# Splitting the first chunk of a fused attention and mixture kernel in two, with the second chunk between the halves

## The chip, the cores and the metric

The kernel runs on one core of a Trainium2 chip. The metric is the device time of one execution in microseconds (us). The core's engines are TensorE (PE, with its weight loads shown as PEld), VectorE (DVE), ScalarE (ACT), GpSimd (POOL) and SyncE (SP, which issues most DMA transfers). Each works through its own queue in order.

## The reference

Three stages follow each other on 4 x 576 = 2304 tokens of width 512:

```python
scores = scale * np.matmul(q, k.transpose(0, 1, 3, 2))     # 4 batches, 8 heads, 576 x 576
scores = np.where(masks[None], scores, -1e9)               # heads 0-3: a band of 32; heads 4-7: every 32nd position
attn = exp(scores - max) / (sum + 1e-9);  x = attn @ v     # -> (2304, 512)
h = x @ w_in;  g = h * sigmoid(1.702 * h);  x = g @ w_out  # first mixture, d_ff 2048
# second mixture: 8 experts with d_ff 1024, each token goes to its top 2
noisy = x @ w_gate + log1p(exp(x @ w_noise)) * noise
out[mask] += top2_w * (relu(x[mask] @ w1[e]) @ w2[e])
```

Everything is float32. Products on TensorE are taken as three products of a rounded part ("hi") and a rest ("lo"): hi*hi, hi*lo, lo*hi.

## The kernel before

**Prologue.** Attention is cut into 64 groups, ordered in parts of 14, 14, 4, 14, 14 and 4; part c is what chunk c of the first mixture needs beyond the earlier parts. "Local" groups are of the banded heads (three masks of 128 x 96), "strided" groups of the others (two masks of 126 x 126 or 72 x 72). A group passes through `scores` (PE; then the mask with its row maximum on DVE, L169), `exps` (ACT, L174), `norms` (L178 and L180 on DVE, then the division: L182 on POOL for the first 28 groups, L186 on DVE for later ones), `transposes` (PE; then an ACT copy, L235 or L240) and `values` (PE, L252 or L262; then hi on ACT, L190, and lo on DVE, L193). The prologue works on groups one after another, a step apart, until all but one of part 0 have left `values`; by then 17 groups have been through `scores`, and six pieces of weights are converted.

**Chunks and slices.** The first mixture then runs in 6 chunks of 384 tokens, each in 16 slices of 128 of the 2048 hidden columns. A slice has 12 matmuls of its first layer (`m1_l1`), a tanh (ACT L416), the gate product (DVE L418), its split into hi (ACT L423) and lo (L425: POOL in chunk 0, DVE later), and 9 matmuls of the second layer of the slice before (`m1_l2`), which add up in the banks PB[2] to PB[4] over the 16 slices. Between the layers come the attention groups of the next part, one per slice: first half of a slice `values`, `transposes`, `scores`, `exps`, then `norms`; second half `values` and `transposes` again. After a chunk, `routing` scales the banks by 0.5 into rows, sends them to DRAM, transposes them, forms the logits and writes the expert lists; its steps are taken from a queue called `fill` at fixed places of the following slices.

**Weights.** Chunk 0 also converts the weights. They arrive as 64-bit words, two 32-bit words each. Of the 16 slices, 0 to 13 come in two wide pieces of 512 words each, 14 and 15 in four small pieces of 256 words each. `w_step` takes up to 512 words: three DVE instructions (`w_bits`, L387, L390, L393) build the float bits, and a step later `w_split` takes hi on ACT (L362) and lo on POOL (L363) and fetches the next raw piece. There are two such steps in each slice, so a slice converts both of its pieces. All four compute engines have their order written out by hand.

**Buffers.** The pool `wp` has 14 buffers. It holds the converted weights of slices 0 to 13, which stay until chunk 5, and the loads and scratch of "early" attention groups (groups 0 to 19 here), up to 8 groups ahead of `scores`. The instruction that first writes a new tile waits until the last reader of the tile that had the buffer is done. Later groups use the pools `ldp` and `tmp`, two ahead. Loads of early groups and of raw weights form one chain on SP, in order. Small pieces use three `stp` and two `tmp` buffers, at most five at a time, and are touched no sooner than LATE half slices after their fetch.

Of the kernel before, what the change touches and what calls it, by code (L numbers as in the profile page):

```python
# [9 lines left out]
F32 = mybir.dt.float32  # L10
F32R = mybir.dt.float32r
BF16 = mybir.dt.bfloat16
I32 = mybir.dt.int32
AF = mybir.ActivationFunctionType
OP = mybir.AluOpType
# [7 lines left out]
DM = H * D  # L23
FF = 2048
NFC = FF // 128
# [4 lines left out]
NCHUNK = N // CH  # L30
TPC = CH // 128
# [18 lines left out]

R_LG = 400
WAIT0 = 14
LATE = 3
REM = 1
CONVAT = (4, 6, 8, 10, 12, 14)
WAIT1 = 15
R_PP = R_LG + 16 * TPC
# [40 lines left out]
def tile_kernel(ctx, tc, qkL, qkS, vL, vS, wm1, wm2, wgn, noise, cst, lst0, out):  # L98
    nc = tc.nc
# [4 lines left out]
    PB = [psum.tile([128, 512], F32, tag=f"pb{i}", name=f"pb{i}") for i in range(8)]  # L104
# [13 lines left out]
    with ExitStack() as main, tc.manual_schedule(engines={mybir.EngineType.PE}):  # L118
# [205 lines left out]
        SPLIT = [[], []]  # L324
# [18 lines left out]
                SMALL.extend((fc, s, o, 256) for o in (0, 256))  # L343

        def w_small():
            while SMALL and len(held) < 5:
                fc, s, o, n = SMALL.pop(0)
                held.append(o)
                if (4 * fc + 2 * s + o // 256) % 5 < 3:
                    raw = stp.tile([128, n, 2], I32, tag="raw", name="raw")  # L350
                else:
                    raw = tmp.tile([128, n, 2], I32, tag="row", name="raw")
                a = 512 * s + o
                chained(raw.rearrange("p n t -> p (n t)"), wm1[fc, :, a:a + n].bitcast(I32))
                PIECES.append((fc, s, raw, o, n))
                born.append(len(done))

        def w_split():

            for fc, s, w32, o, n in SPLIT.pop(0):  # L360
                hi, lo = W1[fc, s]
                nc.scalar.copy(hi[:, o:o + n], w32)  # L362
                nc.gpsimd.tensor_sub(lo[:, o:o + n], w32, hi[:, o:o + n].bitcast(F32))  # L363
                if n < 512:
                    held.pop()
                else:
                    w_raw(fc + 2, s)
            w_small()
            SPLIT.append([])
            done.append(0)  # L370

        def w_step():
            left = 512
            while PIECES and left:
                fc, s, raw, o, n = PIECES[0]
                if n < 512:
                    if len(done) < born[0] + LATE:
                        return
                    born.pop(0)
                PIECES.pop(0)  # L380
                left -= n
                yield from w_bits(fc, s, raw, o, n)

        def w_bits(fc, s, raw, o, n):
            t = tmp.tile([128, n], I32, tag="cv", name="cv", bufs=1)
            low, high = raw[:, :, 0], raw[:, :, 1]
            nc.vector.tensor_scalar(t, high, 3, 0x3FFFFFFF,  # L387
                                    op0=OP.logical_shift_left, op1=OP.bitwise_and)
            yield
            nc.vector.scalar_tensor_tensor(low, low, 29, t,  # L390
                                           op0=OP.logical_shift_right, op1=OP.bitwise_or)
            yield
            nc.vector.scalar_tensor_tensor(low, high, -0x40000000, low,  # L393
                                           op0=OP.bitwise_and, op1=OP.bitwise_or)
            SPLIT[-1].append((fc, s, low.bitcast(F32), o, n))
            yield


        GT = {}
        LASTMM = [None]  # L400

        def m1_l1(c, fc, mid, conv):
            w = W1[fc, 0]
# [17 lines left out]

        def m1_split(c, t, g):
            nc.scalar.copy(g[:, 0], t)  # L423
            eng = nc.vector if c else nc.gpsimd
            eng.tensor_sub(g[:, 1], t, g[:, 0].bitcast(F32))  # L425

        def m1_l2(c, fc, mid):
            w = W1[fc, 1]
            g = GT.pop((c, fc))
            for t in range(TPC):  # L430
                if t == 1:
                    mid()
                o = PB[2 + t]
                a = slice(128 * t, 128 * t + 128)
                nc.tensor.matmul(o, g[:, 0, a], w[0], start=(fc == 0), stop=False)  # L435
                nc.tensor.matmul(o, g[:, 0, a], w[1], start=False, stop=False)  # L436
                m = nc.tensor.matmul(o, g[:, 1, a], w[0], start=False, stop=(fc == NFC - 1))  # L437
            LASTMM[0] = m.ins


# [1 line left out]

        def routing(c, tb, lb, wait=3):
            last = c == NCHUNK - 1
            if last:
                rows = wp.tile([128, TPC, DM], F32, tag="w", name="rows")
                xts = wp.tile([128, TPC, 4, 128], F32, tag="w", name="x2ts")
                row = [rows[:, j, :] for j in range(TPC)]
                xt = [xts[:, j] for j in range(TPC)]
            else:  # L450
                row = [tmp.tile([128, DM], F32, tag="row", name="row") for j in range(2)]
                row.append(stp.tile([128, DM], F32, tag="raw", name="row"))
                xt = [stp.tile([128, 4, 128], F32, tag="raw", name="x2t") for j in range(TPC)]
            for j in range(TPC):
                if j == 1:
                    nc.vector.tensor_scalar(row[j], PB[2 + j], 0.5, None, op0=OP.mult)
                else:
                    nc.scalar.mul(row[j], PB[2 + j], 0.5)
                n = TPC * c + j
                nc.sync.dma_start(x2d[DUMP + 128 * n:DUMP + 128 * n + 128, :], row[j])  # L460
            for j in range(TPC + 1):
                yield
                if j:
                    r = R_LG + 16 * (j - 1)
                    for kc in range(4):
                        nc.tensor.matmul(PB[lb][:, r:r + 16], xt[j - 1][:, kc], wg[:, kc],
                                         start=(kc == 0), stop=(kc == 3))
                if j < TPC:
                    bank = PB[tb[j % len(tb)]]
                    for kc in range(4):  # L470
                        nc.tensor.transpose(bank[:, 128 * kc:128 * kc + 128], row[j][:, 128 * kc:128 * kc + 128],
                                            ident)
                    nc.scalar.copy(xt[j], bank.rearrange("p (k t) -> p k t", t=128))

            lgs = one.tile([128, TPC + 2, 16], F32, tag="lgs", name="lgs")
# [212 lines left out]
        parts = [groups(0, (0, 1)), locals_of(0, (2,)) + groups(1, (0,)), locals_of(1, (1, 2)),  # L688
                 groups(2, (0, 1)), locals_of(2, (2,)) + groups(3, (0,)), locals_of(3, (1, 2))]
        upto = [sum(map(len, parts[:k + 1])) for k in range(len(parts))]  # L690
        att = Attention(sum(parts, []), 20, upto[1])
        att.limit = upto[1]
        att.load(5)
        w_raw(0, 0)
# [45 lines left out]
        def drain():  # L740
            while fill:
                step()
# [4 lines left out]
                att.norms()  # L747
                att.transposes([6])

        seq = [(c, fc) for c in range(NCHUNK) for fc in range(NFC)]  # L750
        for i, (c, fc) in enumerate(seq):
            if fc == 0:
                if c:
                    drain()
                for k in {2: (3, 4), 3: (5,)}.get(c, ()):
                    xtile(k)
                if 0 < c < len(parts):
                    finish(c)
                if c + 1 < len(parts):
                    att.limit = upto[c + 1]  # L760
            conv = w_step()
            t, g = m1_l1(c, fc, step, conv)
            att.values([7])
            att.transposes([6])
            next(conv, None)
            att.scores([5])
            next(conv, None)
            m1_split(c, t, g)
            att.exps()
            for _ in conv:  # L770
                pass
            w_split()
            conv = w_step()
            att.norms(conv)
            if c == 3 and fc in (4, 6, 8, 10, 12):
                clear(x2d, 64 * fc - 256, 1)
            if c == 0 and fc == 12:
                chained(lst.rearrange("(p n) t -> p (n t)", p=128),
                        lst0.rearrange("(p n) t -> p (n t)", p=128), True)
            if c == 4 and fc % 2:  # L780
                clear(out, CH * (fc // 2), min(TPC, NT + NBLK - TPC * (fc // 2)))
            if c == NCHUNK - 1 and fc == 6:
                drain()
                e_list(0, 0, NA // 128, nc.gpsimd)
                fill.append(e_part(0, 0, N + DUMP - CH, wait=WAIT0))
            if c == NCHUNK - 1 and fc >= 8:
                w2_load(fc - 8)
            if i:
                m1_l2(*seq[i - 1], step)
                if fc == 0:  # L790
                    fill.insert(0, routing(c - 1, [6], 7))
            att.values([7], conv)
            next(conv, None)
            att.transposes([6])
            att.load()
            for _ in conv:
                pass
            w_split()
            if (c, fc) == (NCHUNK - 2, NFC - 1):
                fine.close()  # L800
        m1_l2(*seq[-1], step)
# [174 lines left out]
```

## Time and profile before

| | |
|---|---|
| median of 3 runs | 1043.58 us (1042.45 to 1044.43) |
| profiled execution, time | 1042.35 us |
| profiled execution, span | 1040.5 us |
| mean granted TensorE clock over the span | 0.982 |
| share of the span busy: PE, PEld, DVE, ACT, POOL | 96%, 85%, 48%, 38%, 23% |

The span runs from the first to the last instruction; the profiled time is 1.85 us longer. A share is a mean over stages that have different limits, so it says little about one stage. L numbers are lines of the kernel. A timeline row gives start, duration, engine, line, operation, output and inputs; durations of neighbours on one engine overlap a little, so that the distance of two starts is the better measure of what an instruction takes.

### The profile page before, as it was taken

To read this page: it belongs to the slowest core of one execution; us is meant where nothing else is said; L and a number is where in the kernel's file an instruction comes from. 1 tells how busy PE (TensorE), PEld (TensorE's weight loads), DVE (VectorE), ACT (ScalarE), POOL (GpSimd) and SP (SyncE) were. 2 spreads that over 40 slices of the span, in tenths; PEclk is the share of its full clock that TensorE was granted. 3 is DMA by queue.
4 is the path that set the end of the run, shared out by engine and by line. 5 is a ranking of instruction groups with operands and counts; after the bars stand their busy time and mean duration, and the time that the engine had idled before them with its cause. 6 is when DMAs were issued, how large, how long until landed. Compare 5 with 4: busy or idle time off the path is not lost. (4 is left out here: it accounts for less than half of the span.)

```text
span 1040.5 us, 16110 instructions
## 1 busy us (share of the span) xinstructions
PE 996.6 (96%) x5804; PEld 885.0 (85%) x5804; DVE 498.7 (48%) x1509; ACT 394.7 (38%) x1075; POOL 236.0 (23%) x212
## 2 busy tenths in 40 slices
PE   6898799999999999999999989999999999999996
PEld 5676688998888888899998879999999899999995
DVE  6999956236545644522564354243333334343310
ACT  6754444234435444323352243233333333333311
POOL 3577630100100200100210423032321305031302
PEclk9699999999999999999999989999999999999998
DMA  8555521011212323501250165263443617163403
GB/s 291 208 181 190 189 74 47 1 63 46 52 53 88 79 80 110 209 1 41 58 157 32 28 179 159 71 133 112 112 135 89 171 63 173 70 135 118 90 5 51
DMA packets 63744, 107.69 MB, mean 103 GB/s; under 512 B 12448, under 2 KB 25888, under 8 KB 63648
## 3 DMA queue, kind: packets, MB, share of 16 engines
q1 hardware_dynamic: 53488, 85.63, 25.9%
q0 software_dynamic: 10176, 21.02, 10.3%
q8 instruction: 46, 0.75, 0.3%
q14 instruction: 34, 0.28, 0.1%
HBM read 84.04 MB, written 22.73 MB: 103 GB/s over the span
## 5 line engine op out<-in xcount | busy, mean ns | idle before, releaser
L641 DVE SCALAR_TENSOR_TENSOR ht<-pb,ht 128x384 fp32r<-128x384 f32 (+1 forms) x128 | 62.5, 488 | 261.2 <-ACT ht L640 261.0
L640 ACT ACTIVATE ht<-pb 128x384 fp32r<-128x384 f32 (+1 forms) x128 | 56.0, 438 | 271.9 <-PE pb L639 270.6
L411 PE MATMUL pb<-xt,w 128*128 128x384 f32 x384 | 136.2, 355 | 0.0
L669 POOL DMA_INDIRECT out<-y,ix x40 | 65.5, 1637 | 294.8 <-ACT y L668 262.8
L413 PE MATMUL pb<-xt,w 128*128 128x384 f32 x384 | 130.4, 340 | 0.0
L412 PE MATMUL pb<-xt,w 128*128 128x384 f32 x384 | 130.2, 339 | 0.0
L653 PE MATMUL pb<-w,ht 128*128 128x512 f32 x320 | 128.5, 402 | 0.0
L654 PE MATMUL pb<-w,ht 128*128 128x512 f32 x320 | 125.9, 393 | 0.0
L655 PE MATMUL pb<-w,ht 128*128 128x512 f32 x320 | 125.7, 393 | 0.0
L549 POOL DMA_INDIRECT lst<-pay,si x36 | 36.2, 1005 | 386.8 <-DVE si L546 332.1
L418 DVE SCALAR_TENSOR_TENSOR th<-th,pb 128x384 f32<-128x384 f32 x96 | 52.9, 551 | 143.3 <-ACT th L416 143.0
L435 PE MATMUL pb<-w,g 128*128 128x512 f32 x288 | 119.2, 414 | 2.5 <-ACT g L423 2.5
L437 PE MATMUL pb<-w,g 128*128 128x512 f32 x288 | 114.6, 398 | 0.6 <-POOL g L425 0.6
L436 PE MATMUL pb<-w,g 128*128 128x512 f32 x288 | 114.0, 396 | 0.0
L416 ACT ACTIVATE th<-pb 128x384 f32<-128x384 f32 x96 | 47.0, 490 | 124.6 <-PE pb L413 122.4
L567 DVE TENSOR_TENSOR w<-raw,w 128x512 fp32r<-128x512 f32 x128 | 83.8, 688 | 11.3 <-ACT w L566 10.7
L637 PE MATMUL pb<-xa,w 128*128 128x384 f32 x256 | 87.0, 340 | 0.0
L639 PE MATMUL pb<-xa,w 128*128 128x384 f32 x256 | 86.4, 338 | 0.0
L638 PE MATMUL pb<-xa,w 128*128 128x384 f32 x256 | 86.0, 336 | 0.0
L423 ACT CAST g<-th 128x384 fp32r<-128x384 f32 x96 | 49.3, 513 | 88.4 <-DVE th L418 88.4
L566 ACT CAST w<-raw 128x512 fp32r<-128x512 f32 x128 | 73.8, 618 | 11.9 <-DMA raw<-wm 11.7
L411 PEld LDWEIGHTS pb<-xt,w 128*128 128x128 f32 x384 | 73.4, 191 | 2.2
(168 smaller groups left out, 2003.5 us busy)
## 6 DMA issues: line engine op xcount, KB each, us to landing
raw<-wm SPq DMA_DIRECT2D x136, 256.0 KB, 3.0
area<-wm SPq DMA_DIRECT2D x28, 512.0 KB, 4.0
out<-zero SPq DMA_DIRECT2D x7, 768.0 KB, 6.9
qk<-qkS SPq DMA_DIRECT2D x28, 189.0 KB, 2.6
qk<-qkL SPq DMA_DIRECT2D x16, 304.0 KB, 3.0
x2d<-row SPq DMA_DIRECT2D x15, 256.0 KB, 2.2
v<-vL SPq DMA_DIRECT2D x16, 192.0 KB, 2.4
att<-qkL SPq DMA_DIRECT2D x8, 304.0 KB, 5.7
```

What stands on the lines that cost most here:

```text
L411: nc.tensor.matmul(ps, w[0][:, a], X[c][:, 0, kc, :], start=(kc == 0), stop=False)
L412: nc.tensor.matmul(ps, w[0][:, a], X[c][:, 1, kc, :], start=False, stop=False)
L413: nc.tensor.matmul(ps, w[1][:, a], X[c][:, 0, kc, :], start=False, stop=(kc == 3))
L435: nc.tensor.matmul(o, g[:, 0, a], w[0], start=(fc == 0), stop=False)
L436: nc.tensor.matmul(o, g[:, 0, a], w[1], start=False, stop=False)
L437: m = nc.tensor.matmul(o, g[:, 1, a], w[0], start=False, stop=(fc == NFC - 1))
L637: nc.tensor.matmul(ps, w[:, 0, a], x[:, 0, kc, :], start=(kc == 0), stop=False)
L638: nc.tensor.matmul(ps, w[:, 0, a], x[:, 1, kc, :], start=False, stop=False)
L639: nc.tensor.matmul(ps, w[:, 1, a], x[:, 0, kc, :], start=False, stop=(kc == 3))
L653: nc.tensor.matmul(o, g[:, 0, a], w[:, 0, 512:], start=(fc == 0), stop=False)
L654: nc.tensor.matmul(o, g[:, 0, a], w[:, 1, 512:], start=False, stop=False)
L655: m = nc.tensor.matmul(o, g[:, 1, a], w[:, 0, 512:], start=False, stop=(fc == NF2 - 1))
```

## The change

The slices run in another order: chunk 0 slices 0 to 7, chunk 1 slices 0 to 15, chunk 0 slices 8 to 15, then chunks 2 to 5 as before (`SEGS`). Slice 7's sums of chunk 0 are set aside, scaled, in three `stp` buffers (`m1_part`) and added when chunk 0 ends. All attention groups of part 1 now have to be through before slice 8 of the sequence, so each of the first 8 slices may take two groups: the second half has a `scores`, `exps` and `norms` of its own. All of part 1 counts as early (28 groups in place of 20) and up to two groups are loaded at a time. The second weight step of a slice is left out except in slices 0, 2, 4 and 6 and from sequence number 18 on. Small pieces use only the two `tmp` buffers and LATE is 2. In `w_bits` the second and third instruction change places, and the result is written as one packed run of words in place of every second word. The lo part L425 of chunk 0's slices 8 to 15 goes to DVE. Routing of chunk 1 comes before that of chunk 0: chunk 1's rows take a buffer of `xtp`, and chunk 0's rows are three DVE sums. The start list is loaded at slice 12 of chunk 1.

```diff
-LATE = 3
+LATE = 2
+HALFC = NFC // 2
+SMALLS = 18
...
-            while SMALL and len(held) < 5:
+            while SMALL and len(held) < 2:
...
-                if (4 * fc + 2 * s + o // 256) % 5 < 3:
-                    raw = stp.tile([128, n, 2], I32, tag="raw", name="raw")
-                else:
-                    raw = tmp.tile([128, n, 2], I32, tag="row", name="raw")
+                raw = tmp.tile([128, n, 2], I32, tag="row", name="raw")
...
+            w32 = raw.rearrange("p n t -> p (n t)")[:, :n]
             nc.vector.tensor_scalar(t, high, 3, 0x3FFFFFFF,
                                     op0=OP.logical_shift_left, op1=OP.bitwise_and)
             yield
-            nc.vector.scalar_tensor_tensor(low, low, 29, t,
+            nc.vector.scalar_tensor_tensor(t, high, -0x40000000, t,
+                                           op0=OP.bitwise_and, op1=OP.bitwise_or)
+            yield
+
+            nc.vector.scalar_tensor_tensor(w32, low, 29, t,
                                            op0=OP.logical_shift_right, op1=OP.bitwise_or)
-            yield
-            nc.vector.scalar_tensor_tensor(low, high, -0x40000000, low,
-                                           op0=OP.bitwise_and, op1=OP.bitwise_or)
-            SPLIT[-1].append((fc, s, low.bitcast(F32), o, n))
+            SPLIT[-1].append((fc, s, w32.bitcast(F32), o, n))
...
+        SEGS = [(0, 0, HALFC), (1, 0, NFC), (0, HALFC, NFC)] + [(c, 0, NFC) for c in range(2, NCHUNK)]
+        FIRST = {(c, a) for c, a, b in SEGS}
+        LAST = {(c, b - 1) for c, a, b in SEGS}
+        PART = []
+
+        def m1_part():
+            for j in range(TPC):
+                p = stp.tile([128, DM], F32, tag="raw", name="part")
+                if j == 1:
+                    nc.vector.tensor_scalar(p, PB[2 + j], 0.5, None, op0=OP.mult)
+                else:
+                    nc.scalar.mul(p, PB[2 + j], 0.5)
+                PART.append(p)
...
-            eng = nc.vector if c else nc.gpsimd
+            eng = nc.vector if c or fc >= HALFC else nc.gpsimd
...
-                nc.tensor.matmul(o, g[:, 0, a], w[0], start=(fc == 0), stop=False)
+                nc.tensor.matmul(o, g[:, 0, a], w[0], start=((c, fc) in FIRST), stop=False)
...
+                if not c:
+                    nc.vector.scalar_tensor_tensor(row[j], PB[2 + j], 0.5, PART[j], op0=OP.mult, op1=OP.add)
...
-        att = Attention(sum(parts, []), 20, upto[1])
+        att = Attention(sum(parts, []), upto[1], upto[1])
...
-        seq = [(c, fc) for c in range(NCHUNK) for fc in range(NFC)]
+        seq = [(c, fc) for c, a, b in SEGS for fc in range(a, b)]
         for i, (c, fc) in enumerate(seq):
+            if i and (c, fc) in FIRST:
+                drain()
...
-            conv = w_step()
+            conv = w_step() if i < HALFC and not i % 2 or i >= SMALLS else iter(())
             att.norms(conv)
...
-                if fc == 0:
-                    fill.insert(0, routing(c - 1, [6], 7))
+                if i == HALFC:
+                    m1_part()
+                elif seq[i - 1] in LAST:
+                    fill.insert(0, routing(seq[i - 1][0], [6], 7))
             att.values([7], conv)
             next(conv, None)
             att.transposes([6])
-            att.load()
+            if i < HALFC:
+                att.scores([5])
+            att.load(2)
             for _ in conv:
                 pass
             w_split()
+            if i < HALFC:
+                att.exps()
+                att.norms()
```

## Rows read from the trace of the kernel before

**Rows 1.** The page's 40 equal slices of the span, busy tenths of DVE.
```profile
DVE  6999956236545644522564354243333334343310
```

**Rows 2.** Busy time in two stretches; columns PE, PEld, DVE, ACT, POOL.
```profile
45.00:140.00 95.00, 80.23 (x465) 66.68 (x465) 92.02 (x200) 46.87 (x144) 65.81 (x56) 0.96 0.49 161
208.00:224.00 16.00, 16.00 (x85) 14.65 (x84) 3.98 (x8) 3.78 (x8) 0.00 (x0) 1.00 0.00 0
```

**Rows 3.** DVE timeline: gate products that mark slices and chunk starts.
```profile
46.15 0.56 DVE L418 SCALAR_TENSOR_TENSOR th<-th,pb 128x384 f32<-128x384 f32 x1 [0.54 <-ACT th L416]
...
99.99 0.54 DVE L418 SCALAR_TENSOR_TENSOR th<-th,pb 128x384 f32<-128x384 f32 x1
...
106.80 0.54 DVE L418 SCALAR_TENSOR_TENSOR th<-th,pb 128x384 f32<-128x384 f32 x1
...
146.26 0.56 DVE L418 SCALAR_TENSOR_TENSOR th<-th,pb 128x384 f32<-128x384 f32 x1 [3.63 <-ACT th L416]
...
190.78 0.56 DVE L418 SCALAR_TENSOR_TENSOR th<-th,pb 128x384 f32<-128x384 f32 x1 [2.49 <-ACT th L416]
...
194.97 0.56 DVE L418 SCALAR_TENSOR_TENSOR th<-th,pb 128x384 f32<-128x384 f32 x1 [2.49 <-ACT th L416]
...
224.27 0.56 DVE L418 SCALAR_TENSOR_TENSOR th<-th,pb 128x384 f32<-128x384 f32 x1 [2.49 <-ACT th L416]
...
313.62 0.56 DVE L418 SCALAR_TENSOR_TENSOR th<-th,pb 128x384 f32<-128x384 f32 x1 [2.94 <-ACT th L416]
...
481.05 0.56 DVE L418 SCALAR_TENSOR_TENSOR th<-th,pb 128x384 f32<-128x384 f32 x1 [2.49 <-ACT th L416]
...
510.23 0.55 DVE L418 SCALAR_TENSOR_TENSOR th<-th,pb 128x384 f32<-128x384 f32 x1 [2.50 <-ACT th L416]
```

**Rows 4.** Waits from 45 to 140 us: total us, times, longest us.
```profile
ACT g L423 <- DVE th L418: 29.0, 13, 3.6
PEld pb L262 <- ACT pt L240: 11.9, 8, 2.5
```

**Rows 5.** DVE timeline inside chunk 0.
```profile
101.73 0.28 DVE L169 CUSTOM_DVE_ANT_0 psd<-pb,cs 126x126 f32<-126x126 f32 x1
...
102.14 1.08 DVE L393 SCALAR_TENSOR_TENSOR area<-area 128x512 int32<-128x512 int32 x1
103.14 0.41 DVE L387 TENSOR_SCALAR cv<-area 128x512 int32<-128x512 int32 x1
103.48 0.15 DVE L178 TENSOR_SCALAR st<-st 126x2 f32<-126x2 f32 x1
103.66 1.74 DVE L390 SCALAR_TENSOR_TENSOR area<-area,cv 128x512 int32<-128x512 int32 x1
...
105.44 0.69 DVE L393 SCALAR_TENSOR_TENSOR area<-area 128x512 int32<-128x512 int32 x1
...
107.26 0.44 DVE L193 TENSOR_TENSOR xt<-pb,xt 128x42 fp32r<-128x42 f32 x2
...
118.28 0.68 DVE L390 SCALAR_TENSOR_TENSOR area<-area,cv 128x512 int32<-128x512 int32 x1
```

**Rows 6.** POOL timeline: prologue, chunk 0 and its end.
```profile
34.70 0.60 POOL L182 TENSOR_TENSOR att<-att,st 126x252 f32<-126x252 f32 x1 [1.64 <-DVE st L180]
...
103.56 1.30 POOL L363 TENSOR_TENSOR w<-area,w 128x512 fp32r<-128x512 f32 x1 [0.89 <-ACT w L362]
...
143.25 1.02 POOL L425 TENSOR_TENSOR g<-th,g 128x384 fp32r<-128x384 f32 x1 [2.15 <-ACT g L423]
```

**Rows 7.** The groups by line: one that reads packed words, mean ns.
```profile
L567 DVE TENSOR_TENSOR w<-raw,w 128x512 fp32r<-128x512 f32 x128 | 83.8, 688 | 11.3 <-ACT w L566 10.7
```

**Rows 8.** SP's own waits up to 150 us: total us, times, longest us.
```profile
SPq L144 <- PE pb L262: 2.8, 1, 2.8
```

**Rows 9.** PE timeline: a first layer's start and the next `values`.
```profile
54.63 0.42 PE L411 MATMUL pb<-xt,w 128*128 128x384 f32 x1
...
56.89 0.57 PE L252 MATMUL pb<-att 96*64 96x64 f32 x12
```

More of the change, by code (lines that the diff above doesn't have):

```diff
@@ L434, in m1_l2 @@
                 a = slice(128 * t, 128 * t + 128)
-                nc.tensor.matmul(o, g[:, 0, a], w[0], start=(fc == 0), stop=False)
+                nc.tensor.matmul(o, g[:, 0, a], w[0], start=((c, fc) in FIRST), stop=False)
                 nc.tensor.matmul(o, g[:, 0, a], w[1], start=False, stop=False)
-                m = nc.tensor.matmul(o, g[:, 1, a], w[0], start=False, stop=(fc == NFC - 1))
+                m = nc.tensor.matmul(o, g[:, 1, a], w[0], start=False, stop=((c, fc) in LAST))
             LASTMM[0] = m.ins
@@ L444, in routing @@
             last = c == NCHUNK - 1
-            if last:
+            if not c:
+                row = PART
+                xt = []
+            elif c == 1:
+                area = xtp.tile([128, 2 * TPC, DM], F32, tag="xt", name="rows1")
+                row = [area[:, j, :] for j in range(TPC)]
+                xt = [area[:, TPC + j, :].rearrange("p (k t) -> p k t", t=128) for j in range(TPC)]
+            elif last:
                 rows = wp.tile([128, TPC, DM], F32, tag="w", name="rows")
@@ L454, in routing @@
             for j in range(TPC):
-                if j == 1:
+                if not c:
+                    nc.vector.scalar_tensor_tensor(row[j], PB[2 + j], 0.5, PART[j], op0=OP.mult, op1=OP.add)
+                elif j == 1:
                     nc.vector.tensor_scalar(row[j], PB[2 + j], 0.5, None, op0=OP.mult)
@@ L472, in routing @@
                                             ident)
+                    if not c:
+                        xt.append(tmp.tile([128, 4, 128], F32, tag="row", name="x2t"))
                     nc.scalar.copy(xt[j], bank.rearrange("p (k t) -> p k t", t=128))
@@ L748, in finish @@
                 att.transposes([6])
-        seq = [(c, fc) for c in range(NCHUNK) for fc in range(NFC)]
+        seq = [(c, fc) for c, a, b in SEGS for fc in range(a, b)]
         for i, (c, fc) in enumerate(seq):
+            if i and (c, fc) in FIRST:
+                drain()
             if fc == 0:
-                if c:
-                    drain()
                 for k in {2: (3, 4), 3: (5,)}.get(c, ()):
@@ L776, in tile_kernel @@
                 clear(x2d, 64 * fc - 256, 1)
-            if c == 0 and fc == 12:
+            if c == 1 and fc == 12:
                 chained(lst.rearrange("(p n) t -> p (n t)", p=128),
```

## The prediction

> **What bounds the kernel now.** The page's 40 slices of the span come first: DVE reads 9 and 6 in the second to fifth slice, some 26 to 130 us, and 5 or less in nearly all that follow [rows 1]. One stretch differs from the rest, so I look at it alone. From 45 to 140 us DVE is busy for 92.0 of 95 us and PE for 80.2; in a plain stretch of chunk 1 PE is busy for all of 16 us and DVE for 4.0 [rows 2]. The stretch is chunk 0.
>
> The gate product, one per slice, is the clock of this stage [rows 3]. Chunk 0 lasts from 46.15 to 146.26, 100.1 us; chunk 1 from there to 224.27, 78.0 us; chunk 2 to 313.62, 89.35 us. A plain slice takes 194.97 - 190.78 = 4.19 us, sixteen of them 67.0. What chunk 0 would take if PE alone set the pace follows from these. Chunk 5 has no attention: its first six slices take 510.23 - 481.05 = 29.2 us, 4.0 over six plain ones, which is a routing. Chunk 1 has a routing and four local groups: 78.0 - 67.0 - 4.0 = 6.9, or 1.73 us a local group. Chunk 2 has ten strided groups more: 11.3, or 1.13 each. Chunk 0 has no routing; 17 of the 28 groups have been through `scores` before it, so it does ten strided groups (11.3), one local group (1.7) and the later half of three local ones (an estimate, 0.87 each: 2.6), 15.7 in all. That makes 82.7, against 100.1: **chunk 0 loses 17.4 us**, and this is the most that the change can bring.
>
> The waits say to whom: ACT waits 29.0 us for the gate product, that is, for DVE to come round to it, and PE's weight loads 11.9 us for a copy of transposed scores on ACT [rows 4]. A steady slice there takes 106.80 - 99.99 = 6.81 us [rows 3]. DVE's own instructions explain only part of it: the second weight instruction takes 0.68 us at 118.28 and 1.74 us at 103.66, where POOL's 1.30 us subtraction started 0.10 us earlier; the third takes 0.69 and 1.08 [rows 5, 6]. DVE and POOL hold each other up. In a slice POOL has two subtractions at 1.30, a split at 1.02 and a division at 0.60 where nothing holds them, 4.22 us [rows 6]; DVE has two pieces at 0.41 + 0.68 + 0.69 and two small ones at 0.15, 3.86 us of instructions that work in SBUF alone [rows 5]. Together 8.08 in 6.81 us: each us of such work costs 0.84 us. The masks, gate product and x split, which read PSUM, go on beside POOL.
>
> **The change part by part.** *The order.* It spreads 32 pieces of weights, with the small ones, over 24 slices in place of 16, and pulls the attention of part 1 into 8 slices. Three stretches replace chunks 0 and 1 (178.1 us together).
>
> *Chunk 1, 16 slices*: 67.0 and four local groups 6.9, no routing: 74.0. It has one wide piece per slice until number 17: 1.78 on DVE and 1.30 on POOL beside 4.0/16 of DVE's time in a plain stretch [rows 2, 5, 6], under the 4.19 of PE. From number 18 the small pieces come two at a time. Two `tmp` buffers mean that a fetch must wait for POOL to be done with the pair before; a late one holds DVE. Four such fetches at up to half a slice, 2.1 us each, give 8.4 at the most; at the least 0. DVE is three quarters idle there [rows 2], so I take 0.
>
> *Second half of chunk 0, 8 slices*: 33.5 and chunk 1's routing 4.0: 37.6. The eight lo parts that go to DVE (some 0.55 each, by the 0.54 of a gate product of the same size [rows 3]) lie in its idle time.
>
> *First half of chunk 0, 8 slices*: 33.5 and the same 15.7 of attention give 49.2 for PE. Twelve pieces are converted here and twelve groups normalized. POOL: 12 x 1.30 + 8 x 1.02 + 12 x 0.60 = 31.0. DVE in SBUF: 12 x 1.78 + 12 x 0.30 = 25.0. Together 55.9, and at 0.84 it is 47.1: on the mean no longer the bound, but by little, and it is uneven. Slices 0, 2 and 4 have two pieces and two groups: (4.82 + 4.16) x 0.84 = 7.6, against 4.19 + 2 x 1.13 = 6.45 on PE; slices 1, 3 and 5 with one piece 5.0, under PE. In slice 6, two pieces, (3.62 + 3.56) x 0.84 = 6.0 against some 5.2. The excess is 3 x 1.12 + 0.9 = 4.3. Between nothing (the light slices make it up) and 4.3 I take 4.3, since every queue is in order and only one slice deep.
>
> The Trainium skill says (GPSIMD Engine Reference, Key points) that POOL shares its SBUF interfaces with VectorE and contends with DVE instructions that have two SBUF inputs or run in a two-port mode. Read as one or the other at any moment, the first half would take at least 55.9 us, and the total would come to 1042.35 - (17.4 - 6.7) = 1031.7, 1032.9 at the median. The trace agrees that they hold each other up and puts the price at 0.84 [rows 3, 5, 6]; the sum goes by the trace.
>
> *Early groups.* With 28 of them `wp` is full where it had room. At the end of slice 0 three buffers hold weights and eleven are held by or promised to groups 14 to 24; what groups 14 and 15 free goes to the loads of 25 and 26. ACT's copy for slice 3's weights then waits until group 16 has left `values` in slice 1, and at the end of slice 1 that for slice 4's weights waits for group 18; in the prologue's step 13 there is a like wait. Behind the copy on ACT stand the exponents of the group just scored; DVE's norms wait for those, and the weight conversion waits behind the norms. Price of one: from nothing to a first layer and `values` on PE, 56.89 - 54.63 + 0.57 = 2.8 us [rows 9]; the one wait for such a buffer that the trace has, SP's for L262, is 2.8 too [rows 8]. PE itself goes on meanwhile, so I take 0.5 each, 1.5; all three whole would be 8.4.
>
> *Packed words.* The DVE instruction that works on every second word takes 0.68 us [rows 5], one of the same size on packed words 0.69 [rows 7]; POOL's 1.30 for 512 and 1.02 for 384 show no price for the step either (2.5 and 2.7 ns an element) [rows 6]. Between 0 and 0 I take 0. The other order of the three instructions: 0.
>
> *Setting aside and adding.* Three reads of the banks at slice 8 lie, as at each end of a chunk, beside the next first layer, 2.3 us long [rows 9]. Chunk 0's rows, three DVE sums at 0.69 (by [rows 7]) = 2.1, just fit under it. Without this cover they would cost 2.1; I take 0. Routing of chunk 0 now lies in chunk 2 as any routing does, in place of chunk 1's, no difference.
>
> **Sum.** First half 49.2 + 4.3 + 1.5 = 55.0, chunk 1 74.0, second half 37.6: 166.6 against 178.1, 11.5 us less. PE sets the pace from chunk 2 on, so the end moves by as much. The profiled execution took 1042.35, so 1030.85; the median of the runs is 1.23 above it: **1032 us**.
>
> **The rivals.** *PE sets the pace in the first half too.* The light slices make up for the heavy ones and the buffer waits vanish: 49.2, 17.4 us less, 1026.2. For it: the mean of 47.1 is under PE's 49.2. Against it: the in-order queues.
>
> *The early groups choke the first half.* All three buffer waits whole: 49.2 + 4.3 + 8.4 = 61.9, 4.6 less, 1039. For it: they stand ahead of DVE's norms. Against: PE has work that doesn't need them.
>
> *Slower: POOL and DVE overlap nowhere in the first half.* More attention per slice puts divisions between the subtractions, so that DVE's PSUM work (0.41 and 0.36 per group [rows 5], 0.46 per gate product, from 106.80 to 107.26 [rows 3, 5]: 12.9 us) finds no POOL work to lie beside. Then 55.9 + 12.9 = 68.8. It decides from 178.1 - 74.0 - 37.6 = 66.5 on; 68.8 is 2.3 slower, 1045.9. Against it: in the steady slice, 1.3 of 8.1 us overlap and DVE's PSUM work comes on top.
>
> **How the numbers follow.** The forecast with a first half of 52 to 58 us (1029 to 1035): 0.50. PE's pace, 49.2 to 52 (1026 to 1029): 0.24. Choking, 58 to 64 (1035 to 1041): 0.17. No change within 0.2%, 2.1 us, about what a measurement of this kernel can tell (64 to 69 us): 0.03. Slower: 0.06. So faster 0.91, same 0.03, slower 0.06. The range 1026 to 1038 takes in the first two and about half of the third, 0.82.
>
> **What would show it.** In the changed profile the first eight gate products should span some 55 us, the next sixteen 74, the next eight 38. DVE's busy share should fall below 9 tenths from about 100 us on. In slices 0, 2 and 4 the distance of gate products should be near 7.6 and in 1, 3 and 5 near 6.5. ACT should wait for PE's `values` just before a weight copy at the ends of slices 0 and 1. A weight instruction on packed words should still take 0.68. I am wrong if the first half is over 58, if the small pieces hold DVE in chunk 1's last slices, or if anything after chunk 2's start moves by another amount than the start itself.

## The result, and the profile after

The changed kernel takes 1033.10 us, the median of 4 runs (1032.41 to 1034.67), beside 1044.01 of the kernel before; the ratio is 0.9897, with an interval of 0.9876 to 0.9918. A later measurement beside other runs of the kernel before gave 0.9893 (0.9877 to 0.9909). The forecast was 1032, by 11.5 us less; the ratio makes it 10.8. The profiled execution took 1032.68 us, with a span of 1030.9, 9.6 less than before.

The page's busy tenths of DVE, the row that answers to [rows 1]:

```profile
DVE  6979864447446544523655253333434343333310
```

The run of four nines is gone: DVE reads 9 in the second and the fourth slice alone, 7 between them, and 8, 6 and 4 after. The gate products (now L433) show the stages, as in [rows 3]:

```profile
45.86 0.55 DVE L433 SCALAR_TENSOR_TENSOR th<-th,pb 128x384 f32<-128x384 f32 x1 [0.55 <-ACT th L431]
...
54.27 0.55 DVE L433 SCALAR_TENSOR_TENSOR th<-th,pb 128x384 f32<-128x384 f32 x1
...
61.94 0.55 DVE L433 SCALAR_TENSOR_TENSOR th<-th,pb 128x384 f32<-128x384 f32 x1
...
97.87 0.54 DVE L433 SCALAR_TENSOR_TENSOR th<-th,pb 128x384 f32<-128x384 f32 x1
...
172.28 0.56 DVE L433 SCALAR_TENSOR_TENSOR th<-th,pb 128x384 f32<-128x384 f32 x1 [0.62 <-ACT th L431]
...
211.20 0.55 DVE L433 SCALAR_TENSOR_TENSOR th<-th,pb 128x384 f32<-128x384 f32 x1 [2.49 <-ACT th L431]
...
301.83 0.56 DVE L433 SCALAR_TENSOR_TENSOR th<-th,pb 128x384 f32<-128x384 f32 x1 [2.93 <-ACT th L431]
```

The first half of chunk 0 takes 97.87 - 45.86 = 52.0 us (55.0 forecast), chunk 1 74.4 (74.0), the second half of chunk 0 38.9 (37.6): 165.3 in place of 178.1. With a start 0.3 earlier, chunk 2 begins 13.1 us sooner than before. Chunk 2 then takes 90.6 in place of 89.35, and chunk 3, by its gate products, 90.4 in place of 89.35. At the end 9.6 us are left.

Busy time of PE, PEld, DVE, ACT and POOL in the first eight slices and in the 24 after them, to be held against [rows 2]:

```profile
45.90:97.90 52.00, 48.68 (x320) 39.83 (x320) 43.96 (x137) 30.62 (x111) 31.95 (x31) 1.00 0.45 144
97.90:211.20 113.30, 111.53 (x625) 98.93 (x624) 69.05 (x196) 44.15 (x109) 26.58 (x25) 1.00 0.25 83
```

PE is idle for 3.3 us of the first 52 and 1.8 of the next 113; before, it was idle for nearly 15 of 95. The waits from 45 to 105 us (engine and line, what for, total us, times, longest) say what is left:

```profile
ACT g L438 <- DVE th L433: 7.6, 8, 1.8
...
PEld pb L264 <- issue: 3.7, 6, 1.1
...
ACT w L361 <- PE pb L254: 2.5, 1, 2.5
```

ACT's wait for the gate product is 7.6 us here; in the kernel before it is 16.9 in the same window, of the 29.0 of [rows 4], which cover 95 us. The third line is new: it is the buffer wait that the prediction placed at the end of slice 0. The ACT timeline of the changed kernel shows it, and what stands behind it:

```profile
51.82 0.62 ACT L361 CAST w<-area 128x512 fp32r<-128x512 f32 x1 [2.51 <-PE pb L254]
52.35 0.40 ACT L176 ACTIVATE att<-att,st 126x126 f32<-126x126 f32 x1
```

and on DVE's timeline:

```profile
53.25 0.58 DVE L180 TENSOR_SCALAR st<-st 126x2 f32<-126x2 f32 x1 [1.84 <-ACT att L176]
```

The weight copy waits 2.51 us for a group's `values`; the exponents come after it in ACT's order, DVE's norms wait 1.84 us for those, and the weight conversion and gate product of slice 1 come behind the norms. At the end of slice 1 the copy at 59.49 us waits 1.69 us in the same way: the profile names a division on POOL, but the `values` of a group end on PE at 59.32, later than it. DVE's norms wait 2.59 us behind this copy. Slices 0 and 1 take 8.4 and 7.7 us (54.27 - 45.86 and 61.94 - 54.27).

From 105 to 175 us these waits belong to the small pieces, which the prediction put at nothing:

```profile
DVE cv L387 <- DMA raw<-wm: 5.1, 3, 3.8
...
PEld pb L450 <- ACT w L361: 1.1, 1, 1.1
...
PE pb L450 <- ACT w L361: 0.8, 1, 0.8
PE pb L451 <- POOL w L362: 0.8, 1, 0.8
```

The last two are nearly all of PE's idle time in these 24 slices: PE waits for the hi part of the last small pieces, and then for their lo part.

### The profile page after: what moved, and what is told of

The parts are those of the page before. It is cut to its first block, busy times and chain, and to the rows that moved or that the text cites. A ratio compares the mean times of both kernels' runs of the same rounds, so it can differ in the third digit from the quotient of the medians.

```text
span 1030.9 us, 16146 instructions
## 1 busy us (share of the span) xinstructions
PE 993.6 (96%) x5804; PEld 881.5 (86%) x5804; DVE 488.9 (47%) x1520; ACT 393.3 (38%) x1075; POOL 219.1 (21%) x204
## 4 chain that ended last, share of the span: by engine, by line
PE 77%; issue 8%; DVE 6%; DMA 5%; ACT 3%; POOL 2%; POOLq 0%; SPq 0%; ACTq 0%; DVEq 0%
PE pb L665 6%; PE pb L663 6%; PE pb L664 6%; PE pb L680 6%; PE pb L679 6%; PE pb L681 6%; PE pb L426 5%; PE pb L428 5%; PE pb L427 5%; PE pb L450 5%; PE pb L452 5%; PE pb L451 5%; PE pb L635 2%; DMA raw<-wm 2%; PE pb L223 2%
## 5 line engine op out<-in xcount | busy, mean ns | idle before, releaser
L451 PE MATMUL pb<-w,g 128*128 128x512 f32 x288 | 113.3, 393 | 0.8 <-POOL w L362 0.8
L433 DVE SCALAR_TENSOR_TENSOR th<-th,pb 128x384 f32<-128x384 f32 x96 | 52.9, 551 | 128.0 <-ACT th L431 122.1
L427 PEld LDWEIGHTS pb<-xt,w 128*128 128x128 f32 x384 | 72.7, 189 | 2.4 <-DVE xt L195 0.2
```

Source lines behind the costliest of these rows:

```text
L427: nc.tensor.matmul(ps, w[0][:, a], X[c][:, 1, kc, :], start=False, stop=False)
```

## The experiments

Twelve kernels ran in three batches of four, each batch on a chip of its own and with its own runs of the kernel before. Every ratio below is against those. Theory: chunk 0 was long because the SBUF work of DVE and POOL, which hold each other up, all fell into 16 slices; the change spreads the conversion and PE sets the pace. The rivals: DVE alone was the bound; or the order alone, the packing or the early groups bring the gain. The stages, all from the starts of gate products in each profile (us); where one gate product moves, time passes from a stage to the next:

| kernel | first half | chunk 1 | second half | the three | chunk 2 | chunk 3 | span |
|---|---|---|---|---|---|---|---|
| changed | 52.0 | 74.4 | 38.9 | 165.3 | 90.6 | 90.4 | 1030.9 |
| a_full | 63.8 | 80.1 | 37.6 | 181.5 | 89.5 | 89.4 | 1044.2 |
| a_old_bits | 51.9 | 74.2 | 38.9 | 164.9 | 89.5 | 89.4 | 1027.1 |
| a_ahead6 | 49.5 | 74.4 | 38.9 | 162.8 | 89.5 | 89.4 | 1024.8 |
| a_load1 | 52.0 | 74.4 | 38.9 | 165.3 | 89.5 | 89.4 | 1027.5 |
| a_lo_dve | 52.5 | 74.1 | 38.9 | 165.5 | 89.5 | 89.4 | 1030.2 |
| a_late3b | 52.0 | 74.1 | 38.6 | 164.8 | 89.5 | 89.4 | 1032.1 |
| a_same | 52.4 | 74.5 | 38.9 | 165.7 | 90.4 | 90.3 | 1031.2 |
| a_six_late | 49.4 | 74.1 | 38.6 | 162.2 | 90.4 | 90.3 | 1029.1 |
| a_pool0 | 53.4 | 72.7 | 37.6 | 163.6 | 90.5 | 90.2 | 1025.6 |
| a_six_full | 61.2 | 80.1 | 37.6 | 178.9 | 90.4 | 90.3 | 1043.3 |

| kernel | chunk 0 | chunk 1 | the two | chunk 2 | chunk 3 | span |
|---|---|---|---|---|---|---|
| before | 100.1 | 78.0 | 178.1 | 89.4 | 89.4 | 1040.5 |
| b_pool0 | 84.1 | 78.0 | 162.1 | 89.4 | 89.4 | 1023.2 |
| b_lo_dve | 98.2 | 78.1 | 176.3 | 89.4 | 89.4 | 1042.1 |

**POOL's subtraction out of the kernel before (b_pool0).**

```diff
-                nc.gpsimd.tensor_sub(lo[:, o:o + n], w32, hi[:, o:o + n].bitcast(F32))
+                nc.gpsimd.memset(lo[:, o:o + n].bitcast(F32), 0.0)
```

> The kernel before, where POOL writes zeros as the lo part of the weights of the first mixture in place of subtracting (so the products with that part are left out in effect; all instructions of the other engines stay). Theory 1 (chunk 0 is long because POOL's SBUF work holds DVE up): POOL 2.7 in place of 4.2 us per slice, the sum (2.7 + 3.9) x 0.84 = 5.5, near PE's pace: chunk 0 some 87 to 90 us, total 1031 to 1034. Theory 2 (DVE's own instructions fill chunk 0): chunk 0 still 100 us, total 1044.

1026.05 us, ratio 0.9821 (0.9784 to 0.9859). Chunk 0 falls from 100.1 to 84.1 us, 1.4 from the 82.7 worked out for PE alone:

```profile
44.09 0.55 DVE L418 SCALAR_TENSOR_TENSOR th<-th,pb 128x384 f32<-128x384 f32 x1 [0.53 <-ACT th L416]
...
128.19 0.55 DVE L418 SCALAR_TENSOR_TENSOR th<-th,pb 128x384 f32<-128x384 f32 x1 [3.63 <-ACT th L416]
```

No DVE instruction was changed. The groups by line show whose time went (count, total us, mean ns of one), first of the kernel before, then of b_pool0:

```profile
L390 DVE SCALAR_TENSOR_TENSOR area<-area,cv 128x512 int32<-128x512 int32 x28 | 34.1, 1220 | 0.2
```

```profile
L390 DVE SCALAR_TENSOR_TENSOR area<-area,cv 128x512 int32<-128x512 int32 x28 | 19.2, 686 | 0.0
...
L363 POOL MEMSET w<- 128x512 f32 (+1 forms) x36 | 17.8, 504 | 0.0
```

The second weight instruction comes from a mean of 1.22 us to 0.69, what it takes where nothing holds it [rows 5]. Theory 1 holds in its mechanism, and theory 2 falls: without POOL's subtractions chunk 0 is 16 us shorter, and DVE's own instructions fit. Its numbers were too cautious (87 to 90 us for chunk 0, a total of 1031 to 1034). In chunk 0 the second weight instruction accounts for 12.4 of the 16 us (30.9 to 18.5 us in all). The rest isn't divided: a memset is also shorter than a subtraction, and the mean granted clock of this stretch was 1.00, in place of 0.97 in the kernel before.

**The lo part of the gate product from POOL to DVE in the kernel before (b_lo_dve).**

```diff
-            eng = nc.vector if c else nc.gpsimd
+            eng = nc.vector
```

> The kernel before, with the lo part of the gate product on DVE in chunk 0 too (0.56 us there in place of 1.02 on POOL). Theory 1 (both engines' SBUF work adds up at 0.84): 7.62 x 0.84 = 6.4 in place of 6.8 us per slice, chunk 0 some 4 us shorter, total 1040. Theory 2 (DVE, 99% busy, is the bound by itself): 0.5 us more per slice, total 1049.

1043.72 us, ratio 0.9986 (0.9970 to 1.0003): no change. The steady slices stay at 6.8 us, and chunk 0 ends 1.9 us sooner, by its last slices. There TensorE's granted clock was 0.59 in the kernel before (132 to 136 us, mostly the lower of its two levels) and 1.00 in b_lo_dve; how much of the 1.9 that is, isn't shown. The steady slices are as long at 1.00 as at the 0.60 that the kernel before had from 92 to 96 us, so the clock isn't what makes them long. Neither theory's number came. The reason can be read from [rows 5] and POOL's timeline of the kernel before: the POOL split that goes was holding the third weight instruction, which took 1.08 at 102.14 in place of 0.69.

```profile
101.20 1.47 POOL L425 TENSOR_TENSOR g<-th,g 128x384 fp32r<-128x384 f32 x1
```

In the groups by line of b_lo_dve the means are now:

```profile
L390 DVE SCALAR_TENSOR_TENSOR area<-area,cv 128x512 int32<-128x512 int32 x28 | 35.9, 1283 | 0.3
L393 DVE SCALAR_TENSOR_TENSOR area<-area 128x512 int32<-128x512 int32 x28 | 20.3, 724 | 0.2
```

The third weight instruction falls to 0.72 on the mean from 0.89 in the kernel before, and the second is held as much as ever. In slices 1 to 4 DVE pays 0.55 per slice for its own split and gets 0.40 of it back, at two weight steps per slice. So the price of POOL work is not 0.84 per us wherever it stands; as far as these rows show, it is the time by which that piece holds the DVE instruction beside it.

**Both weight steps in every slice (a_full), and the same with 6 groups ahead (a_six_full).**

```diff
-            conv = w_step() if i < HALFC and not i % 2 or i >= SMALLS else iter(())
+            conv = w_step()
```

> The changed kernel with both weight steps in every slice, as before the change; the new order of slices stays. Theory 1 (DVE and POOL, by the 0.84 us per us of SBUF work, set the pace where two pieces meet two groups): slices 0 to 5 at 7.6 us and 6 and 7 at 6.0, the first eight slices 4 us longer than in the changed kernel (56 in place of 52), the total some 1037. Theory 2 (the order alone brings the gain, the halved rate nothing): first eight slices still 52, total 1033.

1045.95 us, ratio 1.0038 (1.0023 to 1.0052): slower than before the change, which rules out theory 2. Theory 1 has the direction, but the first half takes 63.8, not 56, and chunk 1 80.1. With the full rate DVE is the bound at the start of chunk 1 too: from 110 to 127 us it is busy for 16.8 of 16.9 us, and PE for 12.0, at a mean granted clock of 0.80. A steady slice of the first half takes 8.0 us, two gate products on DVE's timeline of a_full:

```profile
79.33 0.22 DVE L180 TENSOR_SCALAR st<-st 126x2 f32<-126x2 f32 x1 [0.74 <-ACT att L176]
...
79.98 0.55 DVE L433 SCALAR_TENSOR_TENSOR th<-th,pb 128x384 f32<-128x384 f32 x1
...
87.99 0.55 DVE L433 SCALAR_TENSOR_TENSOR th<-th,pb 128x384 f32<-128x384 f32 x1
```

At the end of each such slice DVE has nothing between its masks and its norms, and stands 0.74 us until ACT has taken the exponents.

> Both weight steps in every slice as in the full-rate run, with early groups 6 ahead. The full-rate run took 63.8 us for the first eight slices where the sum of SBUF work gave 56. Theory 1 (2.5 of the excess are buffer waits, the rest is DVE's wait for the exponents, 0.7 at the end of a slice): slices 0 and 1 at 7.5 to 8, the others at 8.1 as there, first eight slices 61 to 62. Theory 2 (the excess is all buffer waits): 57.

1046.43 us, ratio 1.0029 (1.0015 to 1.0043). The first half is 61.2, slices 0 and 1 7.1 and 7.9, the others up to 8.1: theory 1. So the new order gives nothing without the lower rate, and the two together take 12.8 us out of the stages. The lower rate without the new order can't be had: chunk 0 would need weights that aren't converted yet.

**The old form of the weight instructions (a_old_bits).**

```diff
-            nc.vector.scalar_tensor_tensor(t, high, -0x40000000, t, ...)
-            nc.vector.scalar_tensor_tensor(w32, low, 29, t, ...)
+            nc.vector.scalar_tensor_tensor(low, low, 29, t, ...)
+            nc.vector.scalar_tensor_tensor(low, high, -0x40000000, low, ...)
```

> The changed kernel with the three weight instructions as they were: old order, result in every second word. Theory 1 (the step of two words costs nothing): DVE's second and third instruction still 0.68 to 0.69 us where nothing holds them, POOL's subtraction 1.30, total within 1 us of the changed kernel. Theory 2 (packed reads and writes are quicker): first eight slices and the total 1 to 3 us longer.

1029.26 us, ratio 0.9879 (0.9863 to 0.9896), beside 1029.98 of a_load1 in its batch; stages as in the changed kernel within 0.3 us. The groups by line, of the changed kernel and of a_old_bits; the third weight instruction, which writes the packed words, is L394 in the first and L393 in the second:

```profile
L362 POOL TENSOR_TENSOR w<-area,w 128x512 fp32r<-128x512 f32 x28 | 37.3, 1335 | 41.7 <-ACT w L361 41.7
L390 DVE SCALAR_TENSOR_TENSOR cv<-area,cv 128x512 int32<-128x512 int32 x28 | 24.5, 874 | 0.0
L394 DVE SCALAR_TENSOR_TENSOR area<-area,cv 128x512 int32<-128x512 int32 x28 | 24.1, 862 | 0.9
```

```profile
L362 POOL TENSOR_TENSOR w<-area,w 128x512 fp32r<-128x512 f32 x28 | 37.4, 1337 | 42.2 <-ACT w L361 41.8 <-DMA att<-vS 0.4
L390 DVE SCALAR_TENSOR_TENSOR area<-area,cv 128x512 int32<-128x512 int32 x28 | 24.7, 881 | 0.0
L393 DVE SCALAR_TENSOR_TENSOR area<-area 128x512 int32<-128x512 int32 x28 | 24.2, 865 | 0.5
```

Packed words bring nothing that shows.

**Early groups 6 ahead in place of 8 (a_ahead6).**

```diff
-                    if i < len(self.gs) and i - self.na < (8 if i < self.early else 2):
+                    if i < len(self.gs) and i - self.na < (6 if i < self.early else 2):
```

> The changed kernel with early groups loaded 6 ahead in place of 8, so that fewer buffers of the weight pool hold attention. Theory 1 (ACT's weight copies wait for buffers that groups hold, and slices 0 and 1 are long for it: 8.4 and 7.7 us): the wait of ACT's copy for values goes, slices 0 and 1 come to 7.6 and 6.5, total 1 to 2 us shorter. Theory 2 (PE has other work meanwhile, or loads come too late at 6): first eight slices 52 as before or longer.

1027.06 us, ratio 0.9861 (0.9845 to 0.9878), the shortest span of all that compute everything. On its timeline the first half runs from 46.59 to 96.05:

```profile
46.59 0.55 DVE L433 SCALAR_TENSOR_TENSOR th<-th,pb 128x384 f32<-128x384 f32 x1 [0.53 <-ACT th L431]
...
96.05 0.55 DVE L433 SCALAR_TENSOR_TENSOR th<-th,pb 128x384 f32<-128x384 f32 x1
```

49.5 us, against 49.2 worked out for PE alone; PE is busy for 48.0 of them, so the 49.2 is an estimate and no floor. Slices 0 and 1 take 7.1 and 6.4. ACT's copies no longer wait for `values`; from 46 to 100 us all that is left for them is

```profile
ACT w L361 <- DVE area L394: 1.2, 1, 1.2
```

The stage shows the 2.5 us plainly; the totals of a_ahead6 and of the other changed kernels of its batch but a_full overlap in their intervals. Its first gate product also comes late, at 46.59, where the kernels with 8 ahead have it at 45.29 to 46.36: at chunk 2's start it is 1.2 us ahead of a_load1. Whether 6 ahead costs something in the prologue isn't shown.

**One load at a time after slice 7 (a_load1), and the changed kernel again (a_same).**

```diff
-            att.load(2)
+            att.load(2 if i < HALFC else 1)
```

> The changed kernel, but with one load at a time after the first eight slices, as before the change. In the changed kernel 13.1 us were saved at chunk 2's start and 9.4 to 9.7 at the end: 1.1 went in slice 7 of chunk 2, 1.1 in slice 7 of chunk 3, 1.4 in chunk 5. Theory 1 (two loads at once make it): the two slices at 5.4 us again, total 2 us shorter. Theory 2 (not the loads): the same two slices at 6.2 us, total the same.

> The changed kernel itself once more, on the chip of the three that follow. Theory 1 (the loss of 1.1 us in slice 7 of chunks 2 and 3 belonged to one execution): these slices at 5.4 us, chunks 2 and 3 at 89.4 us each, span some 1028 to 1029. Theory 2 (it belongs to the kernel): 90.5 us each again.

a_load1: 1029.98 us, ratio 0.9886 (0.9869 to 0.9902), chunks 2 and 3 at 89.5 and 89.4. But a_old_bits and a_ahead6, which load two at a time, have the same 89.5 in the same batch. a_same: 1032.65 us, chunks 2 and 3 at 90.4 and 90.3 again, and so have all the other three kernels of its batch. The loss goes with the batch, not with the edit: theory 1 of a_load1 falls, though its 5.4 us came. In a_same theory 2's number came, but not its cause: a_six_late has only edits that a_ahead6 and a_late3b have too, and these two don't lose the time.

**The lo part on DVE in the first eight slices too (a_lo_dve).**

```diff
-            eng = nc.vector if c or fc >= HALFC else nc.gpsimd
+            eng = nc.vector
```

> The changed kernel with the lo part of the gate product on DVE in the first eight slices too. Theory 1 (added SBUF work of both engines): 8 x 0.46 x 0.84 = 3.1 us less of it, of which PE's pace lets 0 to 2 show: first eight slices 50 to 52, total 1031 to 1033. Theory 2 (DVE alone): 8 x 0.56 more, first eight slices 54 to 56, total 1036.

1031.87 us, ratio 0.9880 (0.9841 to 0.9920), first half 52.5, 0.5 more than in the changed kernel, which slice 8 gives back (5.6 for 6.2): no gain, as in b_lo_dve, and neither theory's stage.

**Small pieces touched later (a_late3b), and with 6 groups ahead (a_six_late).**

```diff
-LATE = 2
+LATE = 3
-SMALLS = 18
+SMALLS = 16
```

> The changed kernel with LATE 3 and SMALLS 16: each small piece is touched half a slice later after its fetch. In the changed kernel DVE's first weight instruction waits 5.1 us in three times for raw weights in slices 19 to 24. Theory 1 (this wait holds the gate product and PE): the wait under 1 us, the stretch from chunk 1's start to chunk 2's 1 to 1.8 us shorter (113.3 to 112), total 1 to 2 us shorter. Theory 2 (DVE has room there): no change.

> The changed kernel with early groups 6 ahead, LATE 3 and SMALLS 16 together. Theory 1 (buffer waits cost 2.5 us in slices 0 and 1, the small pieces 0.6): 3 us shorter than the changed kernel on the same chip. Theory 2 (one of the two hides the other): 2.5 us or less.

a_late3b: 1033.69 us, ratio 0.9886 (0.9849 to 0.9923). The wait for raw weights is gone from the list, but chunk 1 and the second half together take 112.8 in place of 113.3, 0.6 less, below theory 1's 1 to 1.8; the total can't show it. a_six_late: 1030.38 us, ratio 0.9869 (0.9848 to 0.9890), beside 1032.65 of a_same, 2.3 less; the three stretches 162.2 against 165.7, 3.5 us less. In the stages the two edits add up.

**POOL's subtraction out of the changed kernel (a_pool0)**, with the edit of b_pool0.

> The changed kernel, where POOL writes zeros as the lo part of the weights of the first mixture in place of subtracting (the products with that part are left out in effect). In the kernel before the same edit took chunk 0 from 100 to 84 us. Theory 1 (the changed order leaves POOL's hold on DVE nearly nothing to cost): 2 us less in the prologue and at most 1 in the first eight slices, which stay at 51 to 52 for the buffer waits; total 2 to 3 us shorter than the changed kernel. Theory 2 (POOL's hold still sets the pace in the first eight slices): 5 us shorter or more.

1027.08 us, ratio 0.9840 (0.9820 to 0.9860), beside 1032.65: 5.6 us, the size that theory 2 gave, but from several places. By the stages against a_same, the prologue ends 2.7 us sooner (first gate product at 43.66 and 46.36), the first half is 1.0 longer, chunk 1 and the second half are 3.1 shorter together (110.3 against 113.4), and chunk 5 is 1.0 shorter. The longer first half is made by the edit itself. In slice 7 POOL runs twelve memsets back to back, which the subtractions did not, and DVE's first weight instruction, 0.41 us where nothing holds it [rows 5], takes 5.31 beside them. From POOL's and DVE's timelines of a_pool0:

```profile
91.14 5.67 POOL L362 MEMSET w<- 128x512 f32 x12
```

```profile
91.78 5.31 DVE L387 TENSOR_SCALAR cv<-area 128x512 int32<-128x512 int32 x1
97.01 0.54 DVE L433 SCALAR_TENSOR_TENSOR th<-th,pb 128x384 f32<-128x384 f32 x1
```

So the stage can't be read as it stands. Slices 0 to 6, ahead of this, take 45.3 us in place of 48.3 in a_same: the subtractions still cost some 2.9 us in the first half. In slices 18 to 24, where the small pieces are converted, they cost 2.2 (29.3 for 31.6).

## Why the prediction held, and where it did not

*What bounds the kernel before.* The prediction read 9 and 6 in [rows 1]; the row has 9 in all four slices, which makes its case stronger. The loss of 17.4 us in chunk 0 is confirmed from two sides: without POOL's subtraction chunk 0 takes 84.1 us, and the reordered first half with 6 groups ahead 49.5 against 49.2. That POOL holds DVE is shown by L390, 1.22 us before and 0.69 without the subtraction. The other direction was read from rows alone: POOL's split takes 1.47 us at 101.20 and 1.02 where nothing holds it.

*The price of 0.84.* It gave the right answer for the mean (47.1 under PE's 49.2) but is no price. Moving 1.02 us from POOL to 0.55 us on DVE should have saved 0.4 us per slice and saved none, and two pieces with two groups took 8.0 us in a_full, not 7.6, because of DVE's wait for the exponents. It was worked out from one order of instructions and holds for that one.

*The first half: 55.0, measured 52.0.* Two terms were mis-sized, in opposite directions. The step "between nothing and 4.3 I take 4.3, since every queue is in order and only one slice deep" is the larger: with the buffer waits away the stage is 0.3 over PE's pace, so the light slices do make up for the heavy ones (7.0 and 6.9 in slices 2 and 4, not 7.6). This isn't for want of any hold: a_pool0 says that the subtractions still cost some 2.9. The buffer waits, taken at 1.5, cost 2.5. Their mechanism and bound (2.8) were right, and two of the three places: the waits of 2.51 and 1.69 us stand in slices 0 and 1, and none of the six weight copies of the prologue waits.

*Chunk 1 and the second half: 111.6, measured 113.3.* "DVE is three quarters idle there, so I take 0" failed: at the small pieces 1.7 us are lost. The loss is where PE waits for the last small pieces, 0.8 us for hi and 0.8 for lo. Fetching them in better time gives back 0.6 and leaves PE 0.4 and 0.3 there; taking POOL's subtraction away gives back 2.2; a_full, which is done with them before, has exactly 37.6 in the second half. The two gains overlap, and how the loss divides between POOL's hold and the short chain of two buffers stays open.

*Packing, setting aside, adding: 0.* The packing is confirmed by a_old_bits. For the others nothing in the changed kernel's stages asks for more, but no run tried them alone; in a_full, where DVE is full, PE waits 2.5 and 1.0 us for the two engines that set the banks aside.

*From chunk 2 on the end moves with the start.* For chunks 2 and 3 it did in the executions of two batches, which kept 89.4 to 89.5. In the profiled execution of the result, 2.3 us went in chunks 2 and 3 and 1.4 in chunk 5 (69.65 us from its first to its last gate product, 68.26 before). Chunk 5 lies between 68.2 and 69.9 in all the kernels, and the time from its last gate product to the end between 490.2 and 494.9 (a_late3b), without a pattern that an edit explains. So it is in part luck that the total came within 1.1 us of the forecast: the stages gave 1.3 us more, with the earlier start 1.6, and the rest took 3.5 back. Of the prediction's three signs of being wrong two came: the small pieces hold DVE, and what follows chunk 2's start moved by another amount than the start.

*The rivals.* The order without the lower rate is slower than the kernel before. PE's pace in the first half, given 0.24, is what one more edit reaches. The choking by early groups is real but 2.5 us large. The slower case didn't come: the first half took 52.0 us, not 68.8. Nor do POOL and DVE simply take turns in SBUF, which would have needed 55.9.

## What to carry to other kernels

Where a stretch is long because two engines get in each other's way, work out what the pace-setting engine alone would need, from a stretch of the same program without the disturbance; this ceiling (17.4 us here) was more reliable than the price for the interference, and the change reached 12.8 of it. When the work was spread out more thinly, an average load below the pace setter's was nearly enough; alternating heavy and light slices evened out. Loading further ahead takes buffers from whoever allocates next: here two loads fewer ahead were worth 2.5 us in that stage, because the instruction that waited for a buffer stood in front of other work in its queue. And a run that takes an engine's work away can bunch what is left: look at its timeline before its stages are believed, as a_pool0 shows.

## What the runs showed of the hardware that was not expected

In four of the twelve kernels, all of one batch, and in the profiled execution of the result, the stretch from the gate product of slice 6 to that of slice 8 in chunks 2 and 3 is 0.9 to 1.1 us longer, in the other eight not at all, whatever the edit. In the profile of the result ACT stands still before slice 7's tanh though the transposes that its copy needs are long done; from the ACT timeline:

```profile
251.38 0.19 ACT L176 ACTIVATION_READ_ACCUMULATOR psd<-psd,st 126x1 f32 x1
...
254.07 0.37 ACT L242 COPY pt<-pb 126x252 f32<-126x252 f32 x1 [2.50 <-PE pb L428]
```

The transposes start at 250.95 on PE and take 0.4; the releaser named is only the last PE work that the profile has before it. What held ACT for 2.5 us, and why it goes with the batch, stays open.

The second surprise is in a_pool0: a DVE instruction with a single input in SBUF was held 5.31 us, until POOL's run of twelve memsets had ended, and did not come in between two of them. In none of the other profiles did this instruction take more than 1.93 us.
